# Attention then MoE on one core: the sink rows of batch 0's streaming values come by loads of their own instead of by copies behind the casts

## The chip, the cores and the metric

The kernel runs on one core of one Trainium2 chip. The metric is the device time of one execution in microseconds (us). The engines are named as in the profile: PE (TensorE matmul) and PEld (its weight loads), DVE (VectorE), ACT (ScalarE), POOL (GpSimd), SP (SyncE, which here only issues DMAs). Sixteen DMA engines move the data; each holds a queue of its own for every engine that issues.

## The reference

Batch 4, 8 heads, 768 positions, head size 64. Heads 0, 2 and 6 are retrieval heads (full causal attention); the other five are streaming heads: a query sees the first 4 keys (the sinks) and the last 64.

```python
stream_keep = causal & (is_sink | in_win)
scores = np.where(mask, scale * q @ k.T, -1e9)
x = softmax(scores) @ v            # then heads side by side: 3072 tokens x 512
h = x @ w_in                       # 512 -> 2048
return (max(h, 0) + alpha * min(h, 0)) @ w_out
```

Inputs and output are float32.

## The kernel before

The work is cut into 16 segments n = 4 * batch + pair. A pair is two heads that fill the 128 rows of one tile together: pair 0 is (2, 6), two retrieval heads; pair 1 is (1, 5) and pair 3 is (3, 7), two streaming heads each; pair 2 is (0, 4), a retrieval and a streaming head. Batch 0 is segments 0 to 3. Every item of work has a short name, and the list `ORDER` at the top of the file, written out in full, is the order in which all of them are issued. Each engine works its own items strictly in that order, so an item that waits holds everything behind it on its engine.

For a segment n the items are: `Lq`, `Lk`, `Lv` (loads, issued from SP), `Cq`, `Ck`, `Cv` (casts from float32 to bf16; in batch 0 mostly on POOL), `Tq`, `Tk` and `tq`, `tk` (transposes on PE and their copies out of PSUM), `S` and `s` (scores on PE, exponentials on ACT), `A` and `a` (the product with the values on PE, division on DVE), `X` and `x` (transposition of the result into `xT`). Behind attention come `P`, `p`, `g` (the first MoE matmul, its relu on ACT and the rest of its activation on DVE) and the second matmul. The MoE weights are loaded from POOL: `wi0` to `wi7` and `wo0` to `wo3`, between POOL's casts.

A streaming head's keys and values are laid out in seven tiles of 128 rows. In batch 0, rows 0 to 3 of every tile are to hold the four sinks, and rows 4 to 127 hold 124 keys of the sequence (tile 6 holds the last 20). `load_rows` fetches tiles 0 to 5 of one head by one DMA of 128 rows x 6 tiles x 64 elements, whose tiles start 124 keys apart (L277), and tile 6 of the streaming heads by one DMA of 24 rows (L282). With this, rows 0 to 3 of tile 0 are the sinks, and rows 0 to 3 of tiles 1 to 6 are keys that belong to the tile before. `sinks` (L342), called by `cast_v` (L391) and `cast_v_head` (L386) right behind the cast, copies the four sink rows of tile 0 over them: one copy for each streaming head, five in all, four on POOL and one on DVE (segment 3's second head).

Later batches do it otherwise: 112 rows a tile from row 4 on (L270) and a load of four rows x seven tiles with a repeated source for the sinks (L273).

SP's DMAs use eight completion semaphores in turn, so that a load is issued only when the load eight places before it has landed. The part of `ORDER` around the change issues on SP, in this order: `Lv1` (three DMAs), `Lq3`, `Lv2` (three), `Lv3` (three), `Lq4`, `Lk4`. On POOL it issues `wi1`, `wi0` (two halves each), `Cq3`, `Cv1`, `Cv2`, `wi6`, `wi7`, `wi5`, `Cv3.0`, `wi4`, `Cq4`. On PE come, in this order, `Tq3`, `A1.0`, `A1.1`, `A2.0`, `X1`, `A3.0`, `A2.1`, `A3.1`, `X2`, `X3`, and then the bulk of the first MoE matmul (L640).

Of the kernel before, what the change touches and what calls it, by code (L numbers as in the profile page):

```python
# [84 lines left out]
def kernel(  # L85
# [13 lines left out]
    nc = tc.nc  # L99
    B, H, S, D = q.shape  # L100
# [4 lines left out]
    fp32 = DT.float32  # L105
    bf16 = DT.bfloat16

    RETR = [1, 0, 1, 0, 0, 0, 1, 0]
    PAIRS = [(2, 6), (1, 5), (0, 4), (3, 7)]
    NSINK = 4  # L110
    NT = 7
    SLOT = 256
    LAY = 4
# [64 lines left out]
    rows = stat.tile([128, NF * 2560], fp32, name="rows")  # L178
# [13 lines left out]
    def slot(n, kind):  # L192
        return n % NF if n < CROSS else SLOTS[kind].index(n) % DEEP[kind]
# [30 lines left out]
    def dram(t, offset, dims):  # L224
        return bass.AP(t.tensor, t.offset + offset, dims)

    def heads(n):
        return PAIRS[n % 4]
# [17 lines left out]
    def load_k(n):  # L246
        if n >= CROSS:
            load_rows(n, k, kf, 1)
            return
        for hh, h in enumerate(heads(n)):  # L250
            T = row_tokens(n, h)
            dst = kf[slot(n, 1)].rearrange("p a b d -> p (a b d)")[:, 6 * D * hh:6 * D * (hh + 1)]

            (nc.scalar if n == hh == 0 else nc.sync).dma_start(
                dst.rearrange("p (x y) -> p x y", y=T * D),
                dram(k, (n // 4 * H + h) * S * D, [[T * D, 128], [128 * T * D, 6 // T], [1, T * D]]))

    def load_v(n):
        load_rows(n, v, vf, 2)

    def load_rows(n, src, bufs, kind):

        dst = bufs[slot(n, kind)]
        for hh, h in enumerate(heads(n)):
            o = (n // 4 * H + h) * S * D
            if n >= LAY and not RETR[h]:

                end = o + 112 * NT * D > B * H * S * D
                nt = NT - end
                nc.sync.dma_start(dst[NSINK:116, 0:nt, hh, :], dram(src, o, [[D, 112], [112 * D, nt], [1, D]]))  # L270
                if end:
                    nc.sync.dma_start(dst[NSINK:100, 6, hh, :], dram(src, o + 672 * D, [[D, 96], [1, D]]))
                (nc.gpsimd if n == 13 and src is k else nc.sync).dma_start(  # L273
                    dst[0:NSINK, :, hh, :], dram(src, o, [[D, NSINK], [0, NT], [1, D]]))
                continue
            step = 128 if RETR[h] else 124
            nc.sync.dma_start(dst[:, 0:6, hh, :], dram(src, o, [[D, 128], [step * D, 6], [1, D]]))  # L277
        if n < LAY and not all(RETR[h] for h in heads(n)):
            hs = [hh for hh in range(2) if not RETR[heads(n)[hh]]]
            apart = (heads(n)[1] - heads(n)[0]) * S * D  # L280
            o = (n // 4 * H + heads(n)[hs[0]]) * S * D + 744 * D
            nc.sync.dma_start(dst[0:24, 6, hs[0]:hs[-1] + 1, :], dram(src, o, [[D, 24], [apart, len(hs)], [1, D]]))  # L282


    ident = const.tile([128, 128], bf16, name="ident")
# [32 lines left out]
    def cast_of(name):  # L318
        return {"P": nc.gpsimd.tensor_copy, "A": nc.scalar.copy, "V": nc.vector.tensor_copy}[name]
# [14 lines left out]
    CV = "PPPPPPVVVVVVVVVV"  # L334
    natq, natk, held = {}, {}, {}

    def sinks(n, rows, of=range(2), copy=nc.gpsimd.tensor_copy):

        for hh in of if n < LAY else ():
            if not RETR[heads(n)[hh]]:  # L340
                vh = rows[0:NSINK, hh, :, 0:D].bitcast(fp32)
                copy(vh[:, 1:7, :], vh[:, 0:1, :].to_broadcast([NSINK, 6, D // 2]))  # L342

    def part_of(buf, hh):
        return buf.rearrange("p a b d -> p (a b d)")[:, 6 * D * hh:6 * D * (hh + 1)]

# [37 lines left out]
    def cast_v_head(n, hh):  # L384
        vv = vb[n % NV]
        cast_of("PV"[hh])(vv[:, :, hh, 0:D], vf[slot(n, 2)][:, :, hh, :])  # L386
        sinks(n, vv.rearrange("p t h c -> p h t c"), [hh], (nc.gpsimd.tensor_copy, nc.vector.tensor_copy)[hh])

    def cast_v(n):
        vv = vb[n % NV]  # L390
        cast_of(CV[n])(vv[:, :, :, 0:D], vf[slot(n, 2)])  # L391
        sinks(n, vv.rearrange("p t h c -> p h t c"))

    def in_order(ap, T):

# [489 lines left out]
    for n in range(NSEG):  # L885
# [5 lines left out]
        if n == 3:  # L891
            for hh in range(2):
                item(f"Cv{n}.{hh}", cast_v_head, n, hh)
        else:
            item(f"Cv{n}", cast_v, n)
# [101 lines left out]
```

## Time and profile before

| | |
|---|---|
| Runs (3) | 222.54 us median, 222.44 to 223.9 |
| Profiled execution, span | 220.4 us, so the median run is 2.1 us above the span |
| Profiled execution, its own time | not told apart from the span by the profile |
| PE busy | 214.5 us, 97% |
| DVE, ACT, POOL busy | 188.0, 145.8, 45.6 us |
| DMA | 35.98 MB, mean 163 GB/s |

The span runs from the first to the last instruction. Busy time is told for each engine; the share of the DMA engines' time is a sum of their packets' times over 16 engines, and can exceed one where packets overlap. Times in the timelines count from the start of the span.

### The profile page before, as it was taken

The page shows a single profiled execution, that of the slowest core. Times are in us where ns is not written, and L with a number is a line of the kernel's source. Part 1 is how long each engine was busy: PE and PEld are TensorE (multiplying, and loading weights), DVE is VectorE, ACT ScalarE, POOL GpSimd, SP SyncE. Part 2 cuts the span into 40 slices and gives each one's busy share as a digit, 9 for nine tenths or more (in the row PEclk, how much of TensorE's full clock was granted, in tenths as well). Part 3 has the DMA queues.
Part 4 walks back from the last instruction along what each step waited for, and adds up shares of the span by engine and source line. Part 5 has one row for each costly group of instructions (what it writes and reads, how often), then busy time and mean ns, then how long its engine had stood idle before and what let it go on. Part 6 is the DMA issues. An engine that isn't in the chain of part 4 may idle for free.

```text
span 220.4 us, 5779 instructions
## 1 busy us (share of the span) xinstructions
PE 214.5 (97%) x2210; PEld 158.0 (72%) x2210; DVE 188.0 (85%) x471; ACT 145.8 (66%) x314; POOL 45.6 (21%) x92
## 2 busy tenths in 40 slices
PE   8989999999999999999999999999999999999993
PEld 7879866765465865577899666757889645888882
DVE  6879849979989897999998998999999767997841
ACT  4789659989999795657953165799783066816230
POOL 6679980620031200000004110100000200001000
PEclk9999999999999999999999999999999999999999
DMA  6999999999999999979999998791004310002124
GB/s 187 319 233 222 307 241 231 227 201 218 205 245 167 259 162 222 198 182 193 211 215 174 228 184 194 176 187 42 4 1 123 103 79 0 0 3 95 51 93 147
DMA packets 89655, 35.98 MB, mean 163 GB/s; under 512 B 76676, under 2 KB 87964, under 8 KB 89628
## 3 DMA queue, kind: packets, MB, share of 16 engines
q1 hardware_dynamic: 83484, 26.35, 59.4%
q0 software_dynamic: 5824, 8.93, 17.8%
q8 instruction: 17, 0.28, 0.5%
q10 hardware_dynamic: 320, 0.34, 0.5%
q14 instruction: 10, 0.08, 0.1%
HBM read 27.58 MB, written 6.29 MB: 154 GB/s over the span
## 4 chain that ended last, share of the span: by engine, by line
PE 92%; DVE 3%; ACT 2%; issue 1%
PE P L640 36%; PE P L718 28%; PE P L595 7%; PE P L660 7%; PE P L473 4%; PE P L814 3%; PE P L456 2%; PE P L406 2%; PE P L466 1%; PE P L620 1%; DVE kT L435 1%; PE P L544 1%; DVE g L652 1%; ACT neg L645 1%; ACT kT L435 0%
## 5 line engine op out<-in xcount | busy, mean ns | idle before, releaser
L640 PE MATMUL P<-xT,w_in_b 128*128 128x512 bf16 (+1 forms) x512 | 89.6, 326 | 0.0
L652 DVE SCALAR_TENSOR_TENSOR g<-neg,oma,P 128x256 bf16<-128x256 f32 (+1 forms) x128 | 71.7, 607 | 11.4 <-ACT neg L645 11.0
L645 ACT ACTIVATE neg<-P 128x512 f32<-128x512 f32 x96 | 55.4, 602 | 30.3 <-PE P L640 15.7
L640 PEld LDWEIGHTS <-w_in_b 128*128 128x128 bf16 x512 | 49.2, 98 | 29.1 <-issue 0.3
L718 PEld LDWEIGHTS <-g 128*128 128x128 bf16 x480 | 45.7, 98 | 8.1 <-issue 0.8
L512 ACT ACTIVATE eR<-P 128x448 bf16<-128x448 f32 (+4 forms) x63 | 37.0, 627 | 4.8 <-PE P L505 2.2
L718 PE MATMUL P<-w_out_b,g 128*128 128x256 bf16 x320 | 39.0, 273 | 0.0
L736 POOL DMA_DIRECT2D out_dram<-ot x14 | 7.6, 545 | 115.6 <-ACT ot L760 37.9
L560 ACT ACTIVATE eS<-P 128x352 bf16<-128x352 f32 x45 | 20.8, 494 | 2.3 <-PE P L473 1.4
L606 DVE TENSOR_TENSOR xn<-P,rcp 128x448 bf16<-128x448 f32 (+1 forms) x32 | 19.4, 607 | 1.1
L571 DVE TENSOR_TENSOR eS<-eS,ms_near 128x352 bf16<-128x352 bf16 x45 | 15.8, 363 | 0.7 <-ACT eS L560 0.6
L660 PE MATMUL P<-w_out_b,g 128*128 128x512 bf16 x64 | 15.8, 379 | 0.2 <-ACT kT L429 0.2
L703 DVE TENSOR_TENSOR g<-g 128x1024 bf16<-128x1024 bf16 x20 | 13.7, 683 | 0.1
L456 PE MATMUL P<-qT,kT 128*128 128x192 bf16 (+14 forms) x68 | 11.1, 251 | 0.2 <-ACT eS L566 0.2
L595 PEld LDWEIGHTS <-eS 128*128 128x128 bf16 x260 | 10.0, 97 | 1.3
L595 PE MATMUL P<-vb,eS 128*128 128x65 bf16 x260 | 10.8, 193 | 0.0
L522 DVE TENSOR_TENSOR eR<-eR,mr_near 128x128 bf16<-128x128 bf16 (+5 forms) x54 | 10.6, 223 | 0.0
L473 PE MATMUL P<-qT,kT 64*128 64x176 bf16 (+10 forms) x164 | 10.4, 249 | 0.0
L718 PE MATMUL P<-w,g 128*128 128x256 bf16 x80 | 10.4, 273 | 0.0
L660 PEld LDWEIGHTS <-g 128*128 128x128 bf16 x64 | 5.6, 97 | 6.3 <-issue 1.1
L595 PE MATMUL P<-vb,eR 128*128 128x65 bf16 x276 | 10.0, 193 | 0.0
L595 PEld LDWEIGHTS <-eR 128*128 128x128 bf16 x276 | 9.4, 97 | 0.6 <-issue 0.2
(130 smaller groups left out, 267.8 us busy)
## 6 DMA issues: line engine op xcount, KB each, us to landing
out_dram<-ot POOLq DMA_DIRECT2D x18, 256.0 KB, 3.2
rows<-in_k_dram SPq DMA_DIRECT2D x21, 192.0 KB
rows<-in_q_dram SPq DMA_DIRECT2D x18, 192.0 KB
rows<-in_v_dram SPq DMA_DIRECT2D x17, 192.0 KB
rows<-in_v_dram SPq DMA_DIRECT2D x14, 196.0 KB
rows<-in_q_dram SPq DMA_DIRECT2D x7, 384.0 KB
w_out_b<-in_moe_w_out_dram POOLq DMA_DIRECT2D x4, 512.0 KB, 15.1
rows<-in_k_dram SPq DMA_DIRECT2D x9, 196.0 KB
```

Source lines behind the costliest of these rows:

```text
L456: nc.tensor.matmul(to, keys, queries, start=True, stop=stop)
L473: nc.tensor.matmul(to, keys[own], queries[own], start=True, stop=True)
L512: nc.scalar.activation(ebuf[n, hh][:, lo:hi].rearrange("p (x c) -> p x c", x=len(parts)), P[:, got[0]:got[0] + len(parts), 0:(hi - lo) // ...
L560: nc.scalar.activation(slots, sc[:, 0:352].rearrange("p (s c) -> p s c", c=176), AF.Exp, scale=scale)
L571: nc.vector.tensor_tensor(slots, slots, ms_near[:, 0:2, :] if m == 0 else ms_near[:, 1:3, :], op=ALU.mult)
L595: nc.tensor.matmul(pav[:, i, :], e[:, o:o + 128], vv[:, j, hh, 0:D + 1], start=(m == 0), stop=(m == len(terms) - 1))
L606: nc.vector.tensor_tensor(xn[n][:, 0:nt, D * hh:D * hh + D], pav[:, :, 0:D], rcp.to_broadcast([128, nt, D]), op=ALU.mult)
L640: nc.tensor.matmul(psg[:, w * i:w * (i + 1)], w_in_b[:, c, 128 * fb:128 * (fb + 1)], xT[:, c, o:o + w], start=(x == 0), stop=(x == 3))
L645: nc.scalar.activation(neg[t, f], bank(held["P", t, f][0]), AF.Relu, scale=-1.0)
L652: nc.vector.scalar_tensor_tensor(g_buf[t % 2][:, fb, 0:w], neg[t, f][:, c], oma[:, fb:fb + 1], bank(got[0])[:, c], op0=ALU.mult, op1=ALU.add)
L660: nc.tensor.matmul(bank(held["O", t, s][0]), g_buf[t % 2][:, f, 128 * s:128 * (s + 1)], w_out_b[:, f, :], start=(f == 0), stop=(f == 15))
L718: nc.tensor.matmul(q_bank(t, u, CHAIN[y]), left[t, u][y][:, f, :], right[y][:, f, :], start=(first and f == 0), stop=(f == 7), skip_group_ ...
```

## The change

In batch 0 the value load of a streaming head leaves rows 0 to 3 out: it is 124 rows x 6 tiles (L277), and the load of tile 6 is 20 rows (L284). Five new loads, one for each streaming head, bring the four sink rows to all seven tiles at once, from a source that is repeated seven times (L286). They are issued from SP behind the other loads of their segment. The function `sinks` and its calls are gone. The lines in the diff's new part are numbered as in the changed file.

```diff
-            step = 128 if RETR[h] else 124
-            nc.sync.dma_start(dst[:, 0:6, hh, :], dram(src, o, [[D, 128], [step * D, 6], [1, D]]))
+            step, first = (128, 0) if RETR[h] else (124, NSINK)
+            nc.sync.dma_start(dst[first:128, 0:6, hh, :],
+                              dram(src, o + first * D, [[D, 128 - first], [step * D, 6], [1, D]]))
         if n < LAY and not all(RETR[h] for h in heads(n)):
             hs = [hh for hh in range(2) if not RETR[heads(n)[hh]]]
             apart = (heads(n)[1] - heads(n)[0]) * S * D
-            o = (n // 4 * H + heads(n)[hs[0]]) * S * D + 744 * D
-            nc.sync.dma_start(dst[0:24, 6, hs[0]:hs[-1] + 1, :], dram(src, o, [[D, 24], [apart, len(hs)], [1, D]]))
+            o = (n // 4 * H + heads(n)[hs[0]]) * S * D
+            both = slice(hs[0], hs[-1] + 1)
+            nc.sync.dma_start(dst[NSINK:24, 6, both, :], dram(src, o + 748 * D, [[D, 20], [apart, len(hs)], [1, D]]))
+            for hh in hs:
+                nc.sync.dma_start(dst[0:NSINK, :, hh, :],
+                                  dram(src, (n // 4 * H + heads(n)[hh]) * S * D, [[D, NSINK], [0, NT], [1, D]]))
...
-    def sinks(n, rows, of=range(2), copy=nc.gpsimd.tensor_copy):
-
-        for hh in of if n < LAY else ():
-            if not RETR[heads(n)[hh]]:
-                vh = rows[0:NSINK, hh, :, 0:D].bitcast(fp32)
-                copy(vh[:, 1:7, :], vh[:, 0:1, :].to_broadcast([NSINK, 6, D // 2]))
...
     def cast_v_head(n, hh):
         vv = vb[n % NV]
         cast_of("PV"[hh])(vv[:, :, hh, 0:D], vf[slot(n, 2)][:, :, hh, :])
-        sinks(n, vv.rearrange("p t h c -> p h t c"), [hh], (nc.gpsimd.tensor_copy, nc.vector.tensor_copy)[hh])
 
     def cast_v(n):
         vv = vb[n % NV]
         cast_of(CV[n])(vv[:, :, :, 0:D], vf[slot(n, 2)])
-        sinks(n, vv.rearrange("p t h c -> p h t c"))
```

## The prediction, as it was put on record

> **What bounds the kernel now.** I began with the page: PE is busy for 97% of the span, and DVE comes next with 85%. Then the busy time by stretches, around the place of the change.
>
> ```profile
> span 220.4 us, 5779 instructions
> PE 214.5 (97%) x2210; PEld 158.0 (72%) x2210; DVE 188.0 (85%) x471; ACT 145.8 (66%) x314; POOL 45.6 (21%) x92
> 16.00:24.00 8.00, 8.00 (x169) 7.52 (x167) 6.83 (x20) 7.02 (x10) 7.42 (x14) 1.00 1.20 252
> 24.00:31.00 7.00, 7.00 (x107) 5.53 (x105) 5.50 (x13) 3.76 (x6) 6.55 (x12) 1.00 1.15 272
> 31.00:46.00 15.00, 15.00 (x110) 9.62 (x107) 11.94 (x29) 13.47 (x25) 6.72 (x18) 1.00 1.19 228
> ```
>
> The columns of the last three rows are the stretch, its length, busy PE, PEld, DVE, ACT, POOL, the granted clock, the share of the DMA engines' time and GB/s. From 16 to 46 us PE has no idle time and the DMA engines have none either (share 1.15 to 1.20). A delay of PE here has nothing to disappear in, and a delay of a load finds no idle DMA engine to catch up with.
>
> Next I read which load is late already: POOL's timeline and the wait of segment 3's first value cast (L386).
>
> ```profile
> 17.75 0.87 POOL L351 CAST g<-rows 128x768 bf16<-128x768 f32 x1
> 18.51 0.98 POOL L391 CAST vb<-rows 128x896 bf16<-128x896 f32 x1
> 19.55 0.63 POOL L342 COPY vb<-vb 4x192 f32<-4x192 f32 x2
> 20.14 0.92 POOL L391 CAST vb<-rows 128x896 bf16<-128x896 f32 x1
> 21.42 1.85 POOL L824 DMA_DIRECT2D w_in_b<-in_moe_w_in_dram  x3
> 22.65 0.62 DVE L606 TENSOR_TENSOR xn<-P,rcp 128x448 bf16<-128x448 f32 x1
> L386 POOLq EVENT_SEMAPHORE  x1: 1422/1422/1422, 22.2 to 22.2; - x1
> 23.72 0.56 POOL L386 CAST vb<-rows 128x448 bf16<-128x448 f32 x1 [0.45 <-DVE xn L606]
> ```
>
> POOL sits in that wait from 22.2 to 23.6 us. The named releaser ended at 22.65 + 0.62 = 23.27, 0.35 us before, so it was something else: this cast reads what `Lv3` brings, the last DMA of which was issued at 17.16. I read the wait as the landing of `Lv3` at 23.6. PE uses the result almost at once, and PE's chain has little room at the other value products:
>
> ```profile
> 19.42 0.34 PE P L406 x6
> 21.22 0.78 PE P L595 x26
> 22.74 0.81 PE P L595 x27
> 25.07 0.40 PE P L595 x13
> ```
>
> These are `Tq3`, `A1.0` with `A1.1` (2 x 13 matmuls), `A2.0` (27) and `A3.0` (13). The cast for `A3.0` ends at 24.28, 0.8 us before its use. So the values of segment 3 are one of the few loads of this kernel whose landing sets PE's pace.
>
> **How a load is spread over the DMA engines.** The change alters row counts: 128 becomes 124, 24 becomes 20, and loads of 4 are added. What a row count does is found by counting packets. A DMA moves its data in packets, and every DMA engine that takes part adds one small packet for the semaphore.
>
> ```profile
> DMA packets 6698, 3.89 MB, mean 244 GB/s; under 512 B 3404, under 2 KB 6697, under 8 KB 6697
> DMA packets 171, 0.26 MB, mean 350 GB/s; under 512 B 0, under 2 KB 171, under 8 KB 171
> rows<-in_v_dram SPq DMA_DIRECT2D x1, 12.0 KB
> ...
> DMA packets 1664, 0.41 MB, mean 179 GB/s; under 512 B 1664, under 2 KB 1664, under 8 KB 1664
> q1 hardware_dynamic: 1664, 0.41, 79.3%
> rows<-in_k_dram SPq DMA_DIRECT2D x1, 196.0 KB
> rows<-in_k_dram SPq DMA_DIRECT2D x1, 168.0 KB
> rows<-in_k_dram SPq DMA_DIRECT2D x2, 7.0 KB
> rows<-in_k_dram SPq DMA_DIRECT2D x1, 24.0 KB
> ```
>
> The first row is the window 0 to 15.95 us, the second 15.2 to 15.95, where no small packet moves, so the count is a clean cut: everything up to `Lv1` is through and `Lq3` is under way. Packets under 512 B are the values' (256 B) and the semaphores'. The values are four loads of 768 packets and `Lv1`'s load of 24 rows (12 KB) with 48: 3120. The other 284 are semaphore packets. Seventeen DMAs of 128 or 16 rows are done by then (2 from ACT; from SP 4 of Q, 7 of K and the 4 of V); with 16 each they give 272, and 12 remain for the load of 24 rows. It ran on 12 engines, not on 16. The second group is the window 139.2 to 141.5 with an idle gap on either side: five loads, 402 KB or 1608 packets of 256 B; of the 56 others 3 x 16 belong to the loads of 112, 112 and 96 rows, which leaves 4 for each load of 4 rows. So 128, 112, 96 and 16 rows run on 16 engines, 24 on 12, 4 on 4: each time the largest number up to 16 that divides the rows. For 124 = 4 x 31 this is 4 engines, and 20 rows get 10. No row of 124 stands in the trace, so this step is an inference; its rival is below.
>
> The Trainium skill has it as a rule (DMA: Bandwidth & Descriptors, "Why a DMA increments its semaphore by 16 and not by 1"): a DMA from SP runs on the largest k up to 16 that divides the slowest dimension on both sides, and 127 partitions run on a single engine. The two counts above agree; by it the sum is the one I make.
>
> **The change part by part.** The price of a packet comes from the same window: 79.3% x 16 x 2.3 us / 1664 = 17.5 ns. Where loads press, it is dearer (window 64.2 to 66.2):
>
> ```profile
> q1 hardware_dynamic: 1780, 0.45, 128.7%
> ```
>
> This gives 128.7% x 16 x 2.0 / 1780 = 23.1 ns, the upper bound. I take 17.5, since twelve engines would stand idle beside the four.
>
> *The five loads of 124 rows.* On each of the four engines a load puts 744 / 4 = 186 packets, before 768 / 16 = 48: +138, five times +690. *The five sink loads* put 28 / 4 = 7 each on the same four: +35. *The loads of 20 rows*: 40 / 10 = 4 where 48 / 12 = 4 stood: nothing. The bytes are the same. On the four engines `Lv3` thus ends 725 x 17.5 ns = 12.7 us later (16.7 at 23.1 ns), as each engine works off its queue in order and had no idle time here. `Lq3` and `Lv2` stand in the same queues and slip by what precedes them: `Lv1` has 290 packets more (5.1 us), `Lv2` 145 (2.5 us).
>
> *What gets ahead of it.* POOL casts `Cq3`, `Cv1` and `Cv2` when their loads land, and issues `wi6`, `wi7`, `wi5` behind `Cv2`. Now that is before `Lv3` is through, with some 380 of its packets left on each of the four engines, and the weight loads come through another queue that shares the engines. Their packets (1 KB) cost, by the window 15.2 to 40:
>
> ```profile
> q0 software_dynamic: 2487, 2.38, 57.9%
> ```
>
> 57.9% x 16 x 24.8 / 2487 = 92 ns. Three loads of 256 KB are 48 packets an engine: 4.4 us before `Lv3` ends. The bounds are 0 (if they lose every turn) and 4.4; I take 4.4, because the share of q0 in that window is as large as that of the rows, so it doesn't lose turns. Together 17.1 us: `Lv3` lands at 23.6 + 17.1 = 40.7 instead of 23.6.
>
> *PE.* `Tq3` slips by `Cq3`, `A2.0` by `Cv2`; both slips (5 to 8 us) are contained in that of `A3.0`, which now starts behind a cast of 0.56 us and a handover of 0.1: 41.4 for 25.07, that is +16.3. Everything behind it on PE, the MoE's first matmul included, moves with it, and POOL's next loads and casts (`wi4`, `Cq4`), queued behind `Cv3.0`, move by as much; since PE has no idle time in the 15 us that follow, none comes back there. I expect no second wait of that size: `Lq4` and what follows have the same packets as before.
>
> *PE's clock after the stall.* PE will have stood still for about 9 us before `A3.0`. The trace shows what a PE that comes from rest does:
>
> ```profile
> 1.06 4.57 PE P L814 x44
> 20.25 0.22 PE P L814 x4
> ```
>
> The same matmul takes 104 ns at the start and 55 ns later. If PE starts cold again, 4.6 us of work run at half pace and cost up to 2.3 us; if not, nothing. I take 1.2. The Trainium skill (TensorE: Matmul & The Clock Gate, "Part 1: The HAM clock gate") says that the array falls to 1.2 GHz after an idle window of about 3.4 us; no row of this trace shows that, and by it the term would be 2.3 and the forecast 241.
>
> *What is taken away.* Five copies of four rows:
>
> ```profile
> 21.13 0.34 POOL L342 COPY vb<-vb 4x192 f32<-4x192 f32 x1
> 24.34 0.34 POOL L342 COPY vb<-vb 4x192 f32<-4x192 f32 x1
> 26.84 0.37 DVE L342 COPY vb<-vb 4x192 f32<-4x192 f32 x1
> ```
>
> On POOL 0.63 + 0.34 before `Cv3.0` only shorten its wait for the landing. The third POOL copy stands behind the cast, before `wi4`; the DVE copy before the division of `A2.1`. If nothing else moved, 0.3 to 0.7 us could come back. In the forecast these go under in the stall.
>
> *Issues on SP.*
>
> ```profile
> 12.56 0.77 SPq L282 DMA_DIRECT2D rows<-in_v_dram  x1
> 14.90 0.51 SPq L282 DMA_DIRECT2D rows<-in_v_dram  x1
> 17.16 0.47 SPq L282 DMA_DIRECT2D rows<-in_v_dram  x1
> ```
>
> A small load costs SP 0.5 us, five 2.5, and each takes one of eight places in flight. The queues of the four engines hide this, since they hold up to 7 us of unfinished packets; without that cover it is 2.5 us on `Lv3`, of which 2.5 - 0.8 = 1.7 reach PE.
>
> Sum: 16.3 + 1.2 = +17.5 on the profiled span, 220.4 + 17.5 = 237.9. The median of the runs is 2.1 us above the span: **240 us**. Low bound of the mechanism: no weight load gets ahead, no cold clock: 12.7 + 23.6 + 0.66 - 25.07 = +11.9, 234.4. High bound: 16.7 + 4.4 + 23.6 + 0.66 - 25.07 + 2.3 = +22.6, 245.1.
>
> **The rivals.**
> *Spread over sixteen (not slower).* A load of 124 rows takes 16 engines, fifteen with eight rows and one with four. Then the packets are as before and only the copies and issues count: 222.5 - 0.5 = 222.0, if `Lv3` lands as before; it decides as soon as a load keeps 15 engines or more. For it: 128, 112, 96 and 4 rows would look the same under "as many as there are rows, up to 16". Against it: 24 rows on 12 engines. The Trainium skill (same page and section) tells of such a split for direct copies issued from GpSimd; these come from SP.
> *Sixteen engines, but places in flight.* Bytes are spread as before, and the fifteen DMAs from `Lv1` to `Lv3` instead of ten starve the engines: SP's 1.7 us on PE, 224.2. Same evidence against.
> *The weights wait.* The four engines are as I say, but `wi6`, `wi7`, `wi5` don't get ahead, or PE stays warm: 234.4 to 236. For it: nothing shows the order of turns between a long queue of 256 B packets and 1 KB packets on one engine.
> *The stall grows.* POOL's lateness makes the remaining weights (`wi4`, `wi2`, `wi3`) late for the MoE matmul as well, at one load's 16 packets x 92 ns = 1.5 us each: 240 + 4.5 = 244.5, or more if SP, held by four full queues, starts `Lq4` to `Lk7` late.
>
> **How the numbers follow.** My forecast 0.60; weights wait 0.16; stall grows 0.16; the two with sixteen engines 0.06 and 0.02. The likeliest case's own range is 234.4 to 245.1; I widen it to 233 to 248 for the stall that grows, and leave the two rivals near 222 outside. About 1% is what a measurement of this kernel can tell from no change. Over 1% faster (below 220.3) needs 2.2 us from copies that sum to 1.7 us, mostly hidden: 0.02. Within 1%: the two rivals with sixteen engines, less that: 0.06. Slower: 0.92.
>
> **What would show it.** In the changed profile: `Cv1` at about 25 for 18.5 and `Cv3.0` (POOL L384) near 40 for 23.72; a PE gap of 7 to 11 us ahead of `A3.0`; a DMA share near a quarter between 20 and 40 us; packet counts that fit 4 engines for 124 rows. The stages behind are the same, shifted. A DMA share still at 1 in that stretch and `Cv3.0` within 1 us of 23.7 would prove me wrong at the spread; a long wait ahead of L640 for weights would show the stall that grows.

## The result and the profile after

| | before | after |
|---|---|---|
| Median of the runs | 222.51 us (222.13 to 223.9) | 234.61 us (233.58 to 236.16) |
| Profiled execution, span | 220.4 us | 232.7 us |

The ratio is 1.0541 (95% interval 1.0505 to 1.0577): the change costs 12.1 us. The forecast was 240.0 us with a range of 233 to 248. The direction, the place and the mechanism were right, the size was 5.4 us too large.

Of the page of the kernel after, the span, the busy times and the granted clock in 40 slices of 5.8 us:

```profile
span 232.7 us, 5782 instructions
PE 219.5 (94%) x2210; PEld 161.9 (70%) x2210; DVE 187.6 (81%) x470; ACT 146.1 (63%) x314; POOL 44.5 (19%) x88
PEclk9999587999999999999999999999999999999999
```

PE works off the same 2210 matmuls, but is busy 5.0 us longer and idle 7.3 us longer (232.7 - 219.5 against 220.4 - 214.5). Together that is the 12.3 us of the span. The digits 5, 8 and 7 between 23 and 41 us say why the same matmuls took longer: PE ran at half pace there for part of the time. Everything outside this stretch looks as before.

POOL's timeline of the kernel after, with the casts and weight issues around the change (the bracket is the idle time before, and what ended it):

```profile
15.47 2.55 POOL L815 DMA_DIRECT2D w_in_b<-in_moe_w_in_dram  x4
23.64 0.83 POOL L349 CAST g<-rows 128x768 bf16<-128x768 f32 x1 [5.61 <-DMA rows<-in_q_dram]
24.40 0.94 POOL L388 CAST vb<-rows 128x896 bf16<-128x896 f32 x1
26.36 0.94 POOL L388 CAST vb<-rows 128x896 bf16<-128x896 f32 x1 [1.02 <-DMA rows<-in_v_dram]
27.24 1.85 POOL L820 DMA_DIRECT2D w_in_b<-in_moe_w_in_dram  x3
35.36 0.56 POOL L384 CAST vb<-rows 128x448 bf16<-128x448 f32 x1 [6.27 <-DMA rows<-in_v_dram]
```

Read it against the rows of before: `Cq3` 17.75 to 23.64, `Cv1` 18.51 to 24.40, `Cv2` 20.14 to 26.36, `Cv3.0` 23.72 to 35.36. Each cast now waits for a transfer. The slip is 6.2 us at `Cv2` and grows to 11.6 us at `Cv3.0`; the three weight loads (27.24) are issued in between.

PE's timeline, the rows that wait and those next to them:

```profile
24.52 0.82 PE L402 MATMUL P<-ident,g 128*128 128x128 bf16 x6 [4.99 <-POOL g L349]
30.46 0.97 PE L591 MATMUL P<-vb,eR 128*128 128x65 bf16 x27
32.36 0.59 PE L636 MATMUL P<-xT,w_in_b 128*128 128x512 bf16 x2
35.97 0.55 PE L591 MATMUL P<-vb,eS 128*128 128x65 bf16 x13 [3.02 <-POOL vb L384]
```

PE stands twice: 4.99 us ahead of `Tq3`, which needs `Cq3`, and 3.02 us ahead of `A3.0`; `A2.0` between them is 7.9 us late (30.46 for 22.58). How the slip reaches the end: `A3.0` and the bulk of the first MoE matmul in PE's timeline of the kernel before; then, of the kernel after, the transfer that ends the wait (a row of the chain of waits) and the bulk in PE's timeline:

```profile
24.90 0.56 PE L595 MATMUL P<-vb,eS 128*128 128x65 bf16 x13
31.12 6.91 PE L640 MATMUL P<-xT,w_in_b 128*128 128x512 bf16 x39
```

```profile
29.49 5.72 DMA rows<-in_v_dram
...
43.80 6.87 PE L636 MATMUL P<-xT,w_in_b 128*128 128x512 bf16 x39
```

`A3.0` starts at 35.97 for 24.90, 11.1 us later. (The prediction's 25.07 is the chain's row, which begins only where the matmul before it ends.) The bulk starts at 43.80 for 31.12, 12.7 us later, so 1.6 us are lost between `A3.0` and the bulk: 7.8 us for 6.2. From there on the two runs are alike: the spans differ by 12.3 us. Busy time by stretches (columns as in the prediction: after the five engines come the granted clock, DMA share and GB/s) shows where the 1.6 are lost:

```profile
24.00:26.00 2.00, 1.48 (x10) 1.15 (x11) 0.00 (x0) 0.62 (x1) 1.34 (x2) 0.50 0.30 68
33.00:36.00 3.00, 0.03 (x2) 0.03 (x1) 0.20 (x1) 0.14 (x1) 0.64 (x2) 1.00 1.16 247
36.00:37.00 1.00, 1.00 (x23) 1.00 (x23) 0.41 (x2) 0.10 (x1) 0.47 (x1) 1.00 1.10 370
37.00:38.00 1.00, 1.00 (x16) 0.98 (x14) 1.00 (x2) 0.66 (x2) 0.70 (x1) 0.61 1.03 365
38.00:39.00 1.00, 1.00 (x10) 0.51 (x8) 0.92 (x3) 0.54 (x1) 1.00 (x3) 0.50 1.09 353
41.00:42.00 1.00, 1.00 (x19) 0.94 (x17) 0.67 (x3) 0.40 (x1) 1.00 (x3) 1.00 1.20 214
```

PE's clock fell twice. The first time, at the end of the wait of 4.99 us, the half pace cost nothing, since PE had to wait for `Cv3.0` in any case. The second time, 1.2 us after `A3.0` had begun, it delayed the matmuls in front of the bulk.

Last, the transfers of the kernel after: packets and the share of each queue (q1 the loads that SP issues, q0 the weights from POOL), first 24.2 to 28 us, then 31 to 35.3 us.

```profile
DMA packets 1047, 0.26 MB, mean 69 GB/s; under 512 B 1047, under 2 KB 1047, under 8 KB 1047
q1 hardware_dynamic: 1047, 0.26, 30.6%
...
DMA packets 1003, 0.96 MB, mean 223 GB/s; under 512 B 195, under 2 KB 1003, under 8 KB 1003
q0 software_dynamic: 663, 0.64, 90.5%
q1 hardware_dynamic: 340, 0.32, 27.1%
```

In the first stretch only value loads move, at 69 GB/s instead of 272 (the prediction's row 24 to 31 us of the kernel before), with less than a third of the engines' time: a few engines work and the others are idle. One engine alone moves 18 GB/s (the run with 127 rows below), so 69 GB/s are about four engines. In the second the weights have come in and take 90.5%.

### The profile page after: what moved, and what is told of

Same layout as the page of the kernel before. It is cut to its first block, busy times and chain, and to the rows that moved or that the text cites. A ratio compares the mean times of both kernels' runs of the same rounds, so it can differ in the third digit from the quotient of the medians.

```text
span 232.7 us, 5782 instructions
## 1 busy us (share of the span) xinstructions
PE 219.5 (94%) x2210; PEld 161.9 (70%) x2210; DVE 187.6 (81%) x470; ACT 146.1 (63%) x314; POOL 44.5 (19%) x88
## 3 DMA queue, kind: packets, MB, share of 16 engines
q0 software_dynamic: 5824, 8.93, 17.5%
## 4 chain that ended last, share of the span: by engine, by line
PE 81%; DMA 6%; issue 4%; SPq 2%; POOL 2%; ACT 2%; DVE 1%; POOLq 0%; DVEq 0%
PE P L636 34%; PE P L714 26%; PE P L656 6%; PE P L591 6%; PE P L469 4%; DMA rows<-in_k_dram 3%; DMA rows<-in_v_dram 2%; PE P L462 1%; PE P L402 1%; SPq L254 1%; POOL w_in_b L815 1%; SPq L277 1%; PE P L452 1%; DVE g L648 1%; DVE xn L602 1%
## 5 line engine op out<-in xcount | busy, mean ns | idle before, releaser
L636 PE MATMUL P<-xT,w_in_b 128*128 128x512 bf16 (+1 forms) x512 | 90.5, 328 | 0.0
L648 DVE SCALAR_TENSOR_TENSOR g<-neg,oma,P 128x256 bf16<-128x256 f32 (+1 forms) x128 | 71.7, 607 | 11.2 <-ACT neg L641 10.7
L641 ACT ACTIVATE neg<-P 128x512 f32<-128x512 f32 x96 | 55.3, 602 | 30.6 <-PE P L636 15.7
L714 PEld LDWEIGHTS <-g 128*128 128x128 bf16 x480 | 45.7, 98 | 8.1 <-issue 0.8
L601 DVE RECIPROCAL rcp<-P 128x7 f32<-128x7 f32 (+1 forms) x32 | 6.2, 195 | 14.1 <-PE P L591 14.0
L591 PE MATMUL P<-vb,eS 128*128 128x65 bf16 x260 | 12.2, 203 | 3.0 <-POOL vb L384 3.0
L591 PEld LDWEIGHTS <-eS 128*128 128x128 bf16 x260 | 11.4, 105 | 4.9 <-issue 3.8
L452 PE MATMUL P<-qT,kT 128*128 128x192 bf16 (+14 forms) x68 | 12.8, 273 | 0.2 <-ACT eS L562 0.2
L407 ACT COPY qT<-P 128x768 bf16<-128x768 bf16 (+1 forms) x8 | 6.4, 796 | 8.8 <-PE P L402 8.5
L562 ACT ACTIVATE eS<-P 128x768 bf16<-128x768 f32 (+1 forms) x10 | 6.4, 650 | 7.8 <-PE P L540 7.8
L469 PE MATMUL P<-qT,kT 64*128 64x176 bf16 (+10 forms) x164 | 10.4, 248 | 0.2 <-DVE xn L602 0.2
L714 PE MATMUL P<-w,g 128*128 128x256 bf16 x80 | 10.4, 273 | 0.0
```

What stands on the lines that cost most here:

```text
L452: nc.tensor.matmul(to, keys, queries, start=True, stop=stop)
L469: nc.tensor.matmul(to, keys[own], queries[own], start=True, stop=True)
L591: nc.tensor.matmul(pav[:, i, :], e[:, o:o + 128], vv[:, j, hh, 0:D + 1], start=(m == 0), stop=(m == len(terms) - 1))
L636: nc.tensor.matmul(psg[:, w * i:w * (i + 1)], w_in_b[:, c, 128 * fb:128 * (fb + 1)], xT[:, c, o:o + w], start=(x == 0), stop=(x == 3))
L641: nc.scalar.activation(neg[t, f], bank(held["P", t, f][0]), AF.Relu, scale=-1.0)
L648: nc.vector.scalar_tensor_tensor(g_buf[t % 2][:, fb, 0:w], neg[t, f][:, c], oma[:, fb:fb + 1], bank(got[0])[:, c], op0=ALU.mult, op1=ALU.add)
```

## The experiments

The questions were, in this order: is it the row count; what rule does it follow; which of the loads costs the time; and what are weights, clock, copies and small loads worth beside it. In the diffs `-` is the kernel named first.

**Row count alone.** The kernel before with loads of 124 rows; same number of loads, the copies kept.

```diff
-            step = 128 if RETR[h] else 124
-            nc.sync.dma_start(dst[:, 0:6, hh, :], dram(src, o, [[D, 128], [step * D, 6], [1, D]]))
+            step, first = (128, 0) if RETR[h] else (124, NSINK)
+            nc.sync.dma_start(dst[first:128, 0:6, hh, :], dram(src, o + first * D, [[D, 128 - first], [step * D, 6], [1, D]]))
+    fill("vsA", vf[1][0:NSINK, 0:6, :, :], 0.0, nc.gpsimd)     # and so for vf[2], vf[3]
```

> The kernel before with the loads of 128 rows in batch 0's streaming heads cut to 124 (rows 4 to 127) and nothing else on the queues: the same number of loads, the copies kept, no sink loads. Rows 0 to 3 of tiles 0 to 5 are set to zero by three memsets ahead of the loads instead of being loaded, so the sinks' values are left out. Theory 1, the row count by itself: five loads on four engines, 690 packets more on each, at the 14.2 ns a packet that the changed kernel shows for four engines alone 9.8 us; the cast of segment 3 at 31 to 35 us, 230 to 235. Theory 2, the number of small loads: nothing but the memsets changes, 222 to 224.

Measured: 234.28 us, ratio 1.0517 (1.0454 to 1.0579). In POOL's timeline `Cv3.0` is nearly as late as in the kernel after (35.36):

```profile
34.31 0.56 POOL L322 CAST vb<-rows 128x448 bf16<-128x448 f32 x1 [4.37 <-issue]
```

So the row count of five loads makes the whole loss. The sink loads and the missing copies have no visible part in it.

**Which row counts?** The same kernel with `first` = 8, 2 and 1: loads of 120, 126 and 127 rows.

```diff
-            step, first = (128, 0) if RETR[h] else (124, NSINK)
+            step, first = (128, 0) if RETR[h] else (124, 8)    # 120 rows; 2: 126 rows; 1: 127 rows
```

> The kernel before, but the five loads of 128 rows x 6 tiles bring only rows 8 to 127 (120 rows); the copies and the number of loads stay as before. Left out: rows 0 to 7 of these tiles are set to zero. Theory 'largest divisor up to 16': 120 = 15 x 8, so 48 packets on each of 15 engines, as many as before on each: 222 to 224, A3.0 within 1.5 us of 25.1. Rival 'a load that does not begin at partition 0, or does not fill the 128 rows, is slow whatever its count': about 234, as with 124 rows alone.

> As the run with 120 rows, but rows 2 to 127 (126 rows); rows 0 and 1 of these tiles are set to zero. Divisor theory: 126 = 14 x 9, 54 packets on each of 14 engines, 6 more a load, 30 in all x 14.2 ns = 0.4 us: 222.5 to 224. Rival 'what is not a power of two or a multiple of eight is slow': about 234.

> As the run with 120 rows, but rows 1 to 127 (127 rows); row 0 of these tiles is set to zero. Divisor theory: 127 is prime, so one engine has all 762 packets of a load, five loads 3810 x 14.2 ns = 54 us: A3.0 at 70 to 80 instead of 25, and a time of 265 to 285. Rival 'a remainder is handed to a last engine, and three rows more cannot do more harm than four': 234 or less.

Measured: 120 rows 223.45 us, ratio 1.0007 (0.9983 to 1.0031); 126 rows 223.53 us, 1.0009 (0.9984 to 1.0033); 127 rows 276.96 us, 1.2407 (1.2337 to 1.2477). Three rows more than 124 cost another 43 us, and four rows less than 124 cost nothing. Neither the bytes, nor the partition where the load begins, nor a remainder can do that; the largest divisor up to 16 (15, 14 and 1) does. The traces confirm it directly. They record every update of a load's semaphore with its time, and each engine that takes part in a load makes one when its share has landed. A load of 128 rows has 16 such updates, one of 126 rows 14, of 120 rows 15, of 24 rows 12, of 20 rows 10, of 4 rows 4, of 127 rows one; the loads of 124 rows of the kernel after have 4 each. (Where fewer than 16 take part, one more update stands right at the issue.) `Cv3.0` with 120 rows and with 126 rows, from POOL's timelines:

```profile
24.74 0.56 POOL L322 CAST vb<-rows 128x448 bf16<-128x448 f32 x1 [0.88 <-DVE xT L561]
```

```profile
25.52 0.56 POOL L322 CAST vb<-rows 128x448 bf16<-128x448 f32 x1 [1.61 <-DVE rcp L541]
```

With 127 rows the same timeline shows one load after the other:

```profile
38.29 0.83 POOL L287 CAST g<-rows 128x768 bf16<-128x768 f32 x1 [20.84 <-DMA rows<-in_q_dram]
49.61 0.93 POOL L327 CAST vb<-rows 128x896 bf16<-128x896 f32 x1 [8.92 <-DMA rows<-in_v_dram]
75.88 0.56 POOL L322 CAST vb<-rows 128x448 bf16<-128x448 f32 x1 [23.12 <-DMA rows<-in_v_dram]
```

And this is one DMA engine alone, its packets from 66 to 73 us, where nothing else moves:

```profile
DMA packets 496, 0.13 MB, mean 18 GB/s; under 512 B 496, under 2 KB 496, under 8 KB 496
q1 hardware_dynamic: 496, 0.13, 8.0%
```

7.0 us / 496 = 14.1 ns from packet to packet. The busy time of a packet is 8.0% x 16 x 7.0 / 496 = 18.1 ns: a packet begins before the one ahead of it has ended, which is also why one engine of 16 (6.25%) shows a share of 8.0%. With 14.1 ns the distance from `Cq3` to `Cv2`, one load of 762 packets, should be 10.7 us; it is 11.3. From `Cv2` to `Cv3.0` lie two loads and 48 weight packets of 92 ns: 21.5 + 4.4 = 25.9; it is 26.3.

**Only segment 3.** Loads of 124 rows for segment 3 alone, those of segments 1 and 2 with 128.

```diff
-            step, first = (128, 0) if RETR[h] else (124, NSINK)
+            step, first = (128, 0) if RETR[h] else (124, NSINK if n == 3 else 0)
```

> As the earlier run with 124 rows alone, but only segment 3's two loads have 124 rows (rows 0 to 3 set to zero); those of segments 1 and 2 have 128. Two loads of 138 packets more are 276 x 14.2 ns = 3.9 us, plus up to 3 us behind weight loads and some cold clock: 226 to 231, with Cq3 and Cv1 where they were before (17.8 and 18.5). Rival 'the loss comes from the first loads, which make Lq3 and Cv1 late': 222 to 224.

Measured: 232.99 us, ratio 1.0475 (1.04 to 1.0551), above the expected 226 to 231. `Cv2` is where it was, and all the same `Cv3.0` is 8.7 us late, for 276 packets worth 3.9 us:

```profile
20.21 0.92 POOL L327 CAST vb<-rows 128x896 bf16<-128x896 f32 x1
32.46 0.56 POOL L322 CAST vb<-rows 128x448 bf16<-128x448 f32 x1 [9.12 <-DMA rows<-in_v_dram]
```

First the two queues from 18.9 to 24.1 us, about while the first of the two loads is under way; then the weights' queue of the kernel before from 18.9 to 23.7 us, while `Lv3` came in there; last the weights' queue of this run from 24.1 to 32.4 us, up to `Cv3.0`:

```profile
q0 software_dynamic: 440, 0.40, 60.1%
q1 hardware_dynamic: 762, 0.19, 18.7%
...
q0 software_dynamic: 447, 0.40, 54.6%
...
q0 software_dynamic: 715, 0.69, 55.3%
```

440 weight packets are 27.5 an engine, at 92 ns 2.5 us; the other 762 are about one load, which has 744, 186 on each of its four engines, at 14.1 ns 2.6 us. The sum is 5.1 of the 5.2 us. These are the weights of `wi1` and `wi0`, and the third row shows that as many moved beside `Lv3` before the change: they are no extra cost. The later weights are: 715 packets are 44.7 an engine, 4.1 us at 92 ns, where up to 3 us were expected. With the 3.9 us of the 276 packets this makes 8.0 of the 8.7 us; the rest is open. The loads of segments 1 and 2 thus add only some 1.3 us to the loss (234.28 against 232.99, which the intervals do not separate), although they hold 3/5 of the extra packets: what counts is by how much the last load without slack slips.

**The weights behind the cast.** The kernel after, with `wi6`, `wi7`, `wi5` issued behind `Cv3.0`.

```diff
-Cv1 ... Cv2 ... wi6 ... wi7 ... wi5 ... Cv3.0
+Cv1 ... Cv2 ... Cv3.0 wi6 wi7 wi5
```

> The changed kernel with the weight loads wi6, wi7, wi5 issued from POOL behind the value cast of segment 3 instead of ahead of it. Theory 1 with weights getting ahead: the last sink load lands near 32 instead of 35.2 us and the product A3.0 starts 3 us earlier; the time falls to 231 to 232 unless the weights are then late for the first MoE matmul, which would give part back (233 to 236). If the weights don't hold up the loads: cast at 35 as now, time 234 to 237.

Measured: 234.64 us, ratio 1.0534 (1.0486 to 1.0582), not the expected 231 to 232. POOL's timeline:

```profile
29.10 0.93 POOL L323 CAST vb<-rows 128x896 bf16<-128x896 f32 x1 [1.95 <-DMA rows<-in_v_dram]
35.18 0.56 POOL L319 CAST vb<-rows 128x448 bf16<-128x448 f32 x1 [5.15 <-DMA rows<-in_v_dram]
```

From `Cv2` to `Cv3.0` are 6.08 us instead of 9.00: the weight loads had cost `Lv3` 2.9 us. The semaphore updates agree: from the last load of 124 rows to the sink load that `Cv3.0` needs are 0.4 us here (34.63 to 35.04) and 3.4 in the kernel after (31.77 to 35.21). The two loads alone are 372 x 14.1 = 5.2. Nothing was won with it: `Cv3.0` itself is at 35.18, as in the kernel after, since `Cv2` came 2.7 us later in this execution. Three of the four engines had brought their share of its load of 124 rows by 26.06, the fourth at 28.69; why that one lagged is open. And PE later waits 0.89 us for a weight that it had not waited for. So the price of the weights is shown, and moving them repaired nothing in these runs.

**The small loads first.** The kernel after, with the load of 20 rows and the sink loads ahead of the loads of 124 rows.

> The changed kernel with the loads of a segment in another order: the load of 20 rows and the sink loads ahead of the loads of 124 rows. Same loads, same rows. In the changed kernel segment 3's loads of 124 rows have landed by 31.8 us, and the cast waits until 35.2 for a sink load that stands behind the MoE weights. Theory 1 with the last step 'small loads caught behind weights': the first cast needs only its own head's 124 rows, about 29 us, and the time falls by 3 to 6 us to 229 to 232. If only the four engines' packets count, the order changes nothing that ends last: 233 to 235. If the weights hold up the long loads instead, 234 or above.

Measured: 237.44 us, ratio 1.0649 (1.0608 to 1.0689), slower than after and not the expected 229 to 232. PE's timeline, and the weights' queue from 30.6 to 41 us:

```profile
41.95 0.87 PE L591 MATMUL P<-vb,eS 128*128 128x65 bf16 x13 [7.00 <-DVE vb L384]
...
q0 software_dynamic: 1041, 1.00, 64.1%
```

`A3.0` comes earlier (32.1 for 36.0), but `A3.1` now waits 7 us for the second head, whose load of 124 rows is last in the queue and is caught by the weights. By the semaphore updates the first head's load had landed at 30.59 and the second's only at 40.94. In these 10.4 us 65 weight packets an engine moved, 6.0 us at 92 ns. This is a second, independent sign that weights delay whatever load of the four engines stands last.

**PE kept warm.** The kernel after, with 50 more matmuls of zeros ahead of `A3.0`.

```diff
+    def keep_warm(n):
+        b = min((b for b in range(8) if age[b] >= 0), key=lambda b: age[b])
+        for i in range(n):
+            nc.tensor.matmul(bank(b)[:, 0:128], busy, busy, start=True, stop=True)
+    item("keep", keep_warm, 50)                                # in ORDER ahead of A3.0
```

> The changed kernel with 50 matmuls of 128 columns on zeros put on PE ahead of A3.0, into the stall, with no effect on any result. In the changed kernel PE stands still from 32.95 to 35.97 us, and from 37.2 on its matmuls take twice as long for some 4 us, which makes the stretch from A3.0 to the bulk of the first MoE matmul 1.8 us longer than before. If the rest is the cause, 1.3 to 2 us come back: 232.5 to 233.5. If the slow stretch has another cause, nothing or, as the matmuls take 2.8 to 5.2 us, up to 2 us more.

Measured: 233.71 us, ratio 1.0464 (1.0414 to 1.0514). PE's timeline:

```profile
32.72 2.95 PE L795 MATMUL P<-busy 128*128 128x128 bf16 x50
37.32 0.55 PE L526 MATMUL P<-vb,eS 128*128 128x65 bf16 x13 [1.65 <-POOL vb L319]
...
43.52 6.87 PE L571 MATMUL P<-xT,w_in_b 128*128 128x512 bf16 x39
```

From `A3.0` to the bulk are 6.2 us, as in the kernel before, against 7.8 after, and the granted clock stays at 1.00 from 37 to 42 us. The cold clock costs 1.6 us. At the medians the gain is 0.9 us, a little less than expected and not clear of noise (the two intervals overlap); in the profiled execution `Cv3.0` came 1.35 us later, at 36.71.

**Copies, places in flight, and fewer loads.** Three edits of the kernel before: without the five copies; with the five sink loads added, into space that is not used; and with the streaming heads' seven tiles in one load of 128 rows, three loads fewer.

```diff
-                copy(vh[:, 1:7, :], vh[:, 0:1, :].to_broadcast([NSINK, 6, D // 2]))
+                pass
```

> The kernel before without the five copies of four rows; nothing replaces them, so rows 0 to 3 of tiles 1 to 6 hold other keys' values in batch 0's streaming heads. This prices the copies alone. Prediction's account: 0.3 to 0.7 us faster than before at the most, 221.8 to 222.5. Rival, the copies set the pace (POOL 1.3 us, DVE 0.4 us): 221 or less.

```diff
+            for hh in hs:
+                nc.sync.dma_start(scrap.rearrange("p (t d) -> p t d", d=D),
+                                  dram(src, (n // 4 * H + heads(n)[hh]) * S * D, [[D, NSINK], [0, NT], [1, D]]))
```

> The kernel before with five sink loads (4 rows x 7 tiles) added behind each segment's value loads, into a place that nobody reads; rows and copies as before. Theory 1: a small load costs SP about 0.5 us and a place in flight; 222.5 to 224. Theory 2, the number of small loads: in the variant with loads of 112 and 12 rows the landings of row loads and weight loads took turns, one load each, so that a small load takes a whole weight load's time (1.5 to 2.2 us): five more of them 225 to 230.

```diff
-            step = 128 if RETR[h] else 124
-            nc.sync.dma_start(dst[:, 0:6, hh, :], dram(src, o, [[D, 128], [step * D, 6], [1, D]]))
+            step, nt = (128, 6) if RETR[h] else (124, NT)
+            nc.sync.dma_start(dst[:, 0:nt, hh, :], dram(src, o, [[D, 128], [step * D, nt], [1, D]]))
```

> The kernel before with fewer loads: a streaming head's values in batch 0 come as 128 rows x 7 tiles by one load, and the loads of 24 rows fall away; rows 24 to 127 of tile 6, formerly zero, hold other values of the input there, which the masks multiply by zero. Three loads fewer, 896 packets instead of 792 a head. If loads take turns with the weights, one load each, fewer loads land earlier: 219 to 222. If only packets count, 5 x 6.5 packets an engine more at 17.5 ns are 0.6 us: 222.5 to 223.5.

Measured: without copies 223.21 us, ratio 1.0025 (1.0 to 1.005); five more loads 223.82 us, 1.002 (0.9982 to 1.0059); seven tiles 223.7 us, 1.0034 (1.0007 to 1.006). What the change meant to save is worth nothing, and what it adds in issues is worth at most 0.6%. No version of these beats the kernel before.

**The change with other row counts.** The kernel after, with rows 16 to 127 as a load of 112 rows, rows 4 to 15 as a load of 12 rows x 7 tiles and a tail of 8 rows.

```diff
-            step, first = (128, 0) if RETR[h] else (124, NSINK)
+            step, first = (128, 0) if RETR[h] else (124, 16)
+            if not RETR[h]:
+                nc.sync.dma_start(dst[NSINK:16, :, hh, :], dram(src, o + NSINK * D, [[D, 12], [step * D, NT], [1, D]]))
```

> The changed kernel, but a streaming head's tiles 0 to 5 come as 112 rows (16 to 127) and rows 4 to 15 of all seven tiles as a load of 12 rows; the last 8 rows of tile 6 as a load of 8. Sink loads stay, no copies. There are five more loads than in the changed kernel, and the bytes are the same. Theory 1, four engines: 112 rows run on 16 engines and put 42 packets on each instead of 186 on four, so the value cast of segment 3 (35.36 us in the changed kernel, 23.72 before) comes back to 24 to 27 us and the time to 222.5 to 226. Theory 2, places in flight: the loss is from the number of small loads on SP, eight in flight; then five more make it worse, 235 to 240.

Measured: 228.68 us, ratio 1.0253 (1.0208 to 1.0298), between the two expectations. Half of the loss is gone, and the other half has another cause. PE's, POOL's and SP's timelines:

```profile
25.20 0.97 PE L593 MATMUL P<-vb,eR 128*128 128x65 bf16 x27 [2.33 <-POOL vb L390]
```

```profile
24.21 0.93 POOL L390 CAST vb<-rows 128x896 bf16<-128x896 f32 x1 [3.87 <-DMA rows<-in_v_dram]
...
26.90 0.60 POOL L386 CAST vb<-rows 128x448 bf16<-128x448 f32 x1
```

```profile
19.31 1.50 SPq L280 DMA_DIRECT2D rows<-in_v_dram  x1
24.18 0.27 SPq L286 DMA_DIRECT2D rows<-in_v_dram  x1
...
25.24 0.39 SPq L240 DMA_DIRECT2D rows<-in_q_dram  x1
```

`Cv3.0` is back within 3.2 us of before, but `Cv2` is 4.1 us late (24.21 for 20.14), and `A2.0` waits 2.33 us for it. SP issues nothing from 20.8 to 24.18 and `Lq4` at 25.24, where before it was issued right behind `Lv3`, at about 17.7; PE then waits 1.37 and 1.01 us for casts of the next segments. Both waits, that of `Cv2` and that of SP for a free place, end with one landing: by the semaphore updates fifteen of sixteen engines had brought their share of segment 2's load of 112 rows by 21.89, the last at 24.16. Why that one lagged is open. Ten more loads than before are in the eight places in flight here, and five alone cost little; places and pressure together may do it, but no run took them apart.

## Why the prediction was right or wrong

- **Four engines for 124 rows: right.** It was an inference from packet counts; 120, 126 and 127 rows confirm the divisor as a rule with three further points, and the semaphore updates count the engines one by one. The Trainium skill (DMA: Bandwidth & Descriptors, "Why a DMA increments its semaphore by 16 and not by 1") states this rule, and the traces agree.
- **The packets: right count, wrong price.** The term that was mis-sized is "79.3% x 16 x 2.3 us / 1664 = 17.5 ns". It is the busy time of a packet; packets overlap, and an engine that runs alone advances by one in 14.1 ns. The 725 packets cost 10.2 instead of 12.7 us. The slip of `Cv2` is no test of the price, though 435 x 14.1 = 6.1 and `Cv2` began 6.2 us later: before the change it had not waited for its load (its row has no bracket). By the semaphore updates `Lv2` landed at 18.9 before and 26.3 after, 7.4 us apart. The forecast of 7.6 is near that by luck, as it left out the weights of `wi1` and `wi0`: they landed at 19.8 to 24.5 before, behind `Lv2`, and at 19.3 to 24.2 after, ahead of it.
- **The weights: right mechanism, 4.4 us forecast, 2.9 measured** (from `Cv2` to `Cv3.0`, with and without them). The 92 ns held in the run with 127 rows. Of the three loads the last, `wi5`, landed only at 36.49, after `Cv3.0` had begun; two loads at 92 ns are 2.9, which fits.
- **`Cv3.0` at 40.7: was 35.36.** Of the 5.3 us, 2.5 are the packet's price and 1.5 the weights. Of the remaining 1.3, a part is that 14.1 ns holds for few engines. With all sixteen busy (the prediction's window 64.2 to 66.2, 1780 packets in 2.0 us) an engine takes 18.0 ns a packet; by this estimate the 48 packets an engine that each of the five loads had before were worth 0.9 us more than at 14.1, which leaves 0.4. No run took that apart.
- **The cold clock: 1.2 taken, bounds 0 to 2.3; 1.6 measured**, after the change and by the run that kept PE warm. It did start cold again.
- **Signs.** `Cv1` at 24.4 (forecast 25) was right. One gap of 7 to 11 us ahead of `A3.0` was not: the 8.0 us are two gaps, since `Tq3` stands ahead of `A3.0` in PE's order and waits for `Cq3`. A DMA share near a quarter from 20 to 40 us was right only where no weights move (24.2 to 28); elsewhere the weights use the idle engines. The packet counts fit: 1047 packets in 3.8 us, at 14.1 ns each, are 3.9 engines.
- **Copies, issues: at nothing, as forecast**, with 1.0025 and 1.002. The rival "the stall grows" did not come: ahead of the bulk, PE of the kernel after waits for no weight.
- **Low bound 234.4**, without weights and clock at 17.5 ns, which is also where the rival "The weights wait" begins: the measured 234.6 is near it by luck. The packets were 2.5 us too dear there and the 1.3 us above come on the same side, while 2.9 for the weights and 1.6 for the clock were left out. The rival is wrong in its mechanism: weights did get ahead, and PE did go cold.

## What to carry to other kernels

Before taking a few rows off a load that SP issues, factor the new row count: the largest divisor up to 16 is the number of DMA engines that carry it, and 120 or 126 rows are as good as 128 where 124 run on four engines and 127 on one. Look for a load's slack before pricing it: here two of five loads made nearly the whole loss. And price a queue by the distance from one packet to the next, not by a packet's busy time, and in the company that it will have: 14.1 ns for one engine alone, 18.0 with all sixteen busy.

## What the runs showed of the hardware that I had not expected

- SP was held while a few engines had long queues. With 124 rows an issue that takes 0.5 us took 5.28, with 127 rows 15.5 for two:

```profile
18.78 5.28 SPq L284 DMA_DIRECT2D rows<-in_v_dram  x1
```

```profile
47.42 15.54 SPq L212 DMA_DIRECT2D rows<-in_v_dram  x2
```

The first row is of the kernel after, the second of the one with 127 rows. It is not the wait for a free place: the load eight places ahead of the first row's had landed at 15.84, and in the run with 112 rows a wait for a place shows as a gap between rows, not as a long row. That the long queues hold SP is a reading, not shown by an edit; the kernel before has an issue of 3.94 us too, at 35.97, with all engines busy. In the kernel after `Lv3` was thus issued from 24.44 us on, where before it was issued from 15.46 on, and `Lq4`, though spread over all engines, only at 30.24.

- A PE gap of 3.02 us (32.95 to 35.97) was enough for half pace, and not at once: the first 13 matmuls still ran at full pace, and by the mean clock of 0.61 between 37 and 38 us the change came at about 37.2, 4.3 us after the gap began. The Trainium skill (TensorE: Matmul & The Clock Gate, "Part 1: The HAM clock gate") speaks of idle windows of about 3.4 us; the trace shows that a gap somewhat below that can do it.
